# Tile-mode work of an attention + MoE kernel, regrouped: half of the next kv products ahead of the outputs, in one visit to the 64x64 tiles

## Chip, cores, metric

One core of one Trainium2 chip. The time is the device time of the slowest (here the only) core in microseconds, medians of several runs. "Slab" is one of nine blocks of 512 tokens; their lengths are read from traces. In the views PE is the tensor engine, PEld its weight loads, DVE the vector engine and ACT the scalar engine; PSUM, in banks 0 to 7, is where PE leaves its sums until another engine copies them out. "MoE products" are those of the reference's last two lines.

## The reference

```python
q_s = softmax(q, axis=-1); k_s = softmax(k, axis=2)          # per head, 8 x 8 heads, 576 x 64
kv  = einsum('bhsd,bhse->bhde', k_s, v)
x   = einsum('bhsd,bhde->bhse', q_s, kv)   -> [4608, 512]
h   = x @ w_in                                                # 512 -> 2048
out = (h * sigmoid(beta * h)) @ w_out                         # 2048 -> 512
```

## The kernel before

A list of operations is built in program order; each operation waits on semaphores for what it reads, writes and, by PSUM bank, touches. An operation signals if some later operation of another engine depends on it:

```python
for k in r:
    deps.extend(self.writer.get(k, ()))
    self.readers.setdefault(k, []).append(op)     # every reader is kept
for k in w:
    for d in self.readers.get(k, ()):             # so a later writer depends on every one
        if d is not op and not self._same(d, op):
            deps.append(d)
...
for op in self.ops:
    for d in op.deps:
        d.inc = True                              # and every one signals
```

Slab t is 64 MoE products x @ w_in, then 64 products with w_out (four groups u of 16), 128x512 each. Between them lie "visits" to the 64x64 tiles of the array, for attention: `kv_a` and `kv_b`, the two halves of kv of batch t+2 (36 products of 65 columns each, in PSUM banks 1 and 2), `out_quads`, the outputs of batch t+1 (8 products of 512 columns, banks 5, 6, 7, 0), and every second slab `outr_quads`, the remainders of two batches (16 products of 64 columns, again in banks 1 and 2).

```python
def block(b, kv):
    out_quads(b, (5, 6, 7, 0))
    if kv:
        kv_a(b + 1)
    else:
        outr_quads(b, (1, 2))
...                                  # (product of the slab after which it comes, what)
elif t == 1:
    todo = spread(outr_steps(1), 94, 95)
    todo += [(95, lambda: kv_a(2)), (103, lambda: kv_b(2)),
             (117, lambda: block(2, True)), (125, lambda: kv_b(3))]
elif t < 7 and t % 2 == 0:
    todo = [(80, lambda: block(t + 1, False))]
    if t + 2 < B:
        todo += [(93, lambda: kv_a(t + 2)), (101, lambda: kv_b(t + 2))]
elif t < 7:
    todo = [(93, lambda: block(t + 1, True)), (101, lambda: kv_b(t + 2))]
```

K and V are double buffered: exponentials of batch b+2 write the buffer that kv of batch b read. So all 72 kv products of batches up to 5 signal; batches 6 and 7 have no successor and signal only where a result is read. Outputs need QT, q after two transposing transfers.

The softmax here doesn't subtract the row's maximum and nothing guards it: scores larger than these inputs give would overflow.

## Time and profile before

| | before |
|---|---|
| time, median of 3 | 283.53 us (283.52 to 283.65) |
| span of the profiled run | 281.8 us |
| PE busy | 273.1 us, 97% |
| slabs 2, 3, 4, 5, 6, 7 | 29.60, 29.35, 29.45, 29.15, 28.41, 27.63 us |

A slab's length is the distance between the starts of two `XT,WIN` groups in the timeline of PE. How to read the rest stands in the prediction.

### The profile page before, as it was taken

How to read it: one execution, taken by the hardware profiler on the slowest of the kernel's cores; microseconds unless marked ns; L12 is line 12 of the kernel's file. 1: busy time of each engine (PE TensorE's matmuls, PEld its weight loads, DVE VectorE, ACT ScalarE, POOL GpSimd, SP SyncE). 2: the span in 40 equal slices, each digit the busy share in tenths (PEclk: the TensorE clock that was granted, in tenths of full speed). 3: DMA queues.
4: the chain of work that ended last, by engine and by line, in shares of the span. 5: the costliest groups of instructions: out<-in, count | busy, mean ns of one | idle time of the engine just before them, and what ended most of it. 6: DMA issues, size and time to landing. Idle time of an engine off the chain costs nothing.

```text
span 281.8 us, 4474 instructions
## 1 busy us (share of the span) xinstructions
PE 273.1 (97%) x1835; PEld 133.2 (47%) x1870; DVE 106.2 (38%) x211; ACT 168.6 (60%) x242; POOL 36.1 (13%) x56
## 2 busy tenths in 40 slices
PE   7899999999999999999999999999999999999995
PEld 3545454445445444544454444444444444444443
DVE  4764686308392337004651454043704100110012
ACT  5767788889467915794479527881761186017500
POOL 6630041116104030300040000000000000000000
PEclk9799999999999999999999999999999999999999
DMA  7999999999999999909970025000710020012022
GB/s 231 384 386 401 387 381 302 379 334 240 262 395 181 333 311 404 108 0 269 341 155 3 2 93 130 0 3 37 171 36 0 29 122 0 0 58 93 0 74 74
DMA packets 42044, 50.10 MB, mean 178 GB/s; under 512 B 20900, under 2 KB 29348, under 8 KB 40872
## 3 DMA queue, kind: packets, MB, share of 16 engines
q1 hardware_dynamic: 41072, 48.77, 57.6%
q10 hardware_dynamic: 952, 1.06, 1.1%
q8 instruction: 14, 0.23, 0.4%
q14 instruction: 6, 0.05, 0.0%
HBM read 36.71 MB, written 9.44 MB: 164 GB/s over the span
## 4 chain that ended last, share of the span: by engine, by line
PE 89%; ACT 4%; issue 2%; DVE 2%; DMA 1%; POOL 0%; ACTq 0%; POOLq 0%
PE PS L390 88%; ACT EQ L320 2%; DMA QF<-in_q_dram 1%; ACT L339 1%; PE PS L388 1%; ACT EK L339 1%; DVE QS L356 0%; POOL EQ L358 0%; ACT EQR L345 0%; ACT XT L540 0%; DVE KVD L428 0%; DVE EQ L358 0%; DVE KVC L527 0%; DVE RC L525 0%; DVE QI L357 0%
## 5 line engine op out<-in xcount | busy, mean ns | idle before, releaser
L723 ACT ACTIVATE GT<-PS,BETA 128x512 bf16<-128x512 f32 x144 | 96.8, 689 | 81.8 <-PE PS L390 81.8
L390 PE MATMUL PS<-WOUT,GT 128*128 128x512 bf16 (+2 forms) x569 | 126.8, 373 | 1.7 <-issue 0.5
L390 PE MATMUL PS<-XT,WIN 128*128 128x512 bf16 x565 | 125.8, 379 | 0.6
L390 PEld LDWEIGHTS PS<-XT,WIN 128*128 128x128 bf16 x576 | 60.6, 106 | 63.0 <-ACT GT L723 0.4
L390 PEld LDWEIGHTS PS<-WOUT,GT 128*128 128x128 bf16 x592 | 55.8, 98 | 63.0
L778 DVE COPY O2S<-PS 128x512 f32<-128x512 f32 x33 | 22.7, 688 | 97.0 <-PE PS L390 96.9
L375 POOL CAST VB<-VF 128x576 bf16<-128x576 f32 x29 | 20.8, 718 | 77.2 <-DMA VF<-in_v_dram 67.3
L356 DVE TENSOR_REDUCE QS<-EQ 128x8 f32<-128x512 bf16 (+1 forms) x22 | 20.0, 911 | 15.7 <-ACT EQ L320 15.7
L540 DVE CAST XT<-PS 128x512 bf16<-128x512 f32 x12 | 7.7, 686 | 33.8 <-PE PS L390 33.8
L320 ACT ACTIVATE EQ<-QF 128x512 bf16<-128x512 f32 x32 | 17.8, 616 | 1.7 <-DMA QF<-in_q_dram 1.5
L339 ACT ACTIVATE EK<-KF 128x1152 bf16<-128x1152 f32 (+1 forms) x16 | 15.9, 1035 | 1.7 <-DMA KF<-in_k_dram 1.5
L358 DVE TENSOR_TENSOR EQ<-EQ,QI 128x1024 bf16<-128x1024 bf16 (+1 forms) x14 | 16.0, 1146 | 0.5
L358 POOL TENSOR_TENSOR EQ<-EQ,QI 128x512 bf16<-128x512 bf16 x8 | 8.3, 1042 | 27.9 <-DVE QI L357 27.5
L390 PEld LDWEIGHTS PS<-VB,EK 64*64 64x64 bf16 x504 | 7.3, 109 | 5.2 <-issue 3.9
L540 ACT CAST XT<-PS 128x512 bf16<-128x512 f32 x12 | 6.3, 577 | 4.8 <-PE PS L390 4.8
L390 PE MATMUL PS<-VB,EK 64*64 64x65 bf16 x504 | 8.8, 195 | 0.0
L723 ACT ACT_TABLE_LOAD x5 | 6.4, 1283 | 0.1
L390 PE MATMUL PS<-XT 128*128 128x512 f32 x6 | 5.0, 1009 | 1.5 <-DVE XT L221 1.5
L332 ACT ACTIVATE EKD<-KF 64x576 bf16<-64x576 f32 (+1 forms) x6 | 5.0, 841 | 1.0 <-DMA KF<-in_k_dram 0.9
L525 DVE RECIPROCAL RC<-PS 128x2 f32<-128x2 f32 x12 | 2.0, 165 | 8.8 <-PE PS L390 8.8
L357 DVE RECIPROCAL QI<-QS 128x8 f32<-128x8 f32 (+1 forms) x22 | 5.0, 226 | 0.8
L339 ACT ACT_TABLE_LOAD x4 | 5.1, 1283 | 0.1
(62 smaller groups left out, 87.3 us busy)
## 6 DMA issues: line engine op xcount, KB each, us to landing
out_dram<-O2S SPq DMA_DIRECT2D x8, 1024.0 KB, 5.1
QF<-in_q_dram SPq DMA_DIRECT2D x30, 256.0 KB, 6.6
KF<-in_k_dram SPq DMA_DIRECT2D x6, 1152.0 KB, 8.5
VF<-in_v_dram SPq DMA_DIRECT2D x6, 1152.0 KB, 11.5
KF<-in_k_dram SPq DMA_DIRECT2D x8, 288.0 KB, 8.4
VF<-in_v_dram SPq DMA_DIRECT2D x8, 288.0 KB, 8.7
WST<-in_moe_w_in_dram SPq DMA_DIRECT2D x8, 256.0 KB, 8.3
O2S<-in_moe_w_in_dram SPq DMA_DIRECT2D x4, 512.0 KB, 11.9
```

The costliest lines, as they stand in the source:

```text
L320: add(ACTE, lambda e, o=o, a=a: e.activation(o, a, ACT.Exp), r=[("qf", i, hp)] if b < 2 else [("qf", i, hp, x) for x in ((2, 3) if hp % 2 ...
L332: add(ACTE, lambda e: e.activation(o, a, ACT.Exp), r=[("kf", i, h) for h in hps], w=[("ek", i, h, e_) for h in hps])
L339: add(ACTE, lambda e: e.activation(o, a, ACT.Exp), r=[("kf", i, h) for h in range(hp, hp + n)], w=[("ekc", i, h) for h in range(hp, hp + n)])
L356: add(DVE, lambda e: e.tensor_reduce(s_, a, AX.X, ALU.add), r=ks, w=[("qs", i, hp0)])
L357: add(DVE, lambda e: e.reciprocal(v_, s_), r=[("qs", i, hp0)], w=[("qi", i, hp0)])
L358: add(eng, lambda e: e.tensor_tensor(a, a, vb, ALU.mult), r=ks + [("qi", i, hp0)], w=ks)
L375: add(eng, lambda e: (e.copy if eng == ACTE else e.tensor_copy)(o, a), r=[("vf", i, hp), ("vone", i)], w=[("vb", i, hp, h) for h in ((0, 1 ...
L388: add(PE, lambda e: e.transpose(o, l, r_), r=r, w=w, bank=[bk])
L390: add(PE, lambda e: e.matmul(o, l, r_, start=start, stop=stop, tile_position=tp), r=r, w=w, bank=[bk])
L540: add(eng, lambda e, eng=eng, bk=bk, hp=hp: (e.copy if eng == ACTE else e.tensor_copy)(XT[i][:, hp, :], PS[bk][:, :]), r=[("ps", bk)], w=[ ...
L723: add(ACTE, lambda e: e.activation(GT[:, f, :], PS[bk][:, :], ACT.Silu, scale=BETA[:, f:f + 1]), r=[("ps", bk), "beta"], w=[("gt", f)], ba ...
L778: add(eng, lambda e: (e.copy if eng == ACTE else e.tensor_copy)(O2S[t % 2][:, u, :], PS[bk][:, :]), r=[("ps", bk)], w=[("o2", t % 2, u)], ...
```

## The change

The intent: fewer visits. In even slabs, outputs with remainders and each half of kv made three visits; now half of kv, outputs and remainders are one, and the other half follows 18 products on. In odd slabs and in slab 1 the number of visits stays and kv goes ahead of the outputs.

```diff
-        def block(b, kv):
+        def block(b):
+            if b + 1 < B:
+                kv_a(b + 1)
             out_quads(b, (5, 6, 7, 0))
-            if kv:
-                kv_a(b + 1)
-            else:
+            if b % 2 and b > 1:
                 outr_quads(b, (1, 2))
@@ t == 1
-                         (117, lambda: block(2, True)), (125, lambda: kv_b(3))]
+                         (116, lambda: block(2)), (124, lambda: kv_b(3))]
@@ t > 1
-            elif t < 7 and t % 2 == 0:
-                todo = [(80, lambda: block(t + 1, False))]
+            elif t < 7:
+                todo = [(94, lambda: block(t + 1))]
                 if t + 2 < B:
-                    todo += [(93, lambda: kv_a(t + 2)), (101, lambda: kv_b(t + 2))]
-            elif t < 7:
-                todo = [(93, lambda: block(t + 1, True)), (101, lambda: kv_b(t + 2))]
+                    todo += [(112, lambda: kv_b(t + 2))]
```

## The prediction

> **What bounds the kernel now**
>
> I read the page's busy shares first, then the chain that ended last, then the tensor engine's timeline from 45 us to the end, then narrow windows of its weight loads and of the vector engine.
>
> ```profile
> PE 273.1 (97%) x1835; PEld 133.2 (47%) x1870; DVE 106.2 (38%) x211; ACT 168.6 (60%) x242; POOL 36.1 (13%) x56
> ...
> PE 89%; ACT 4%; issue 2%; DVE 2%; DMA 1%; POOL 0%; ACTq 0%; POOLq 0%
> ```
>
> TensorE (PE) is busy for 97% of the span and is 89% of the chain; ACT, the next engine, is at 60%. A gain must come out of PE's own stream. The timeline of PE over slab 4, and the two ends of slab 7, which has no attention work in it:
>
> ```profile
> 136.31 13.98 PE L390 MATMUL PS<-XT,WIN 128*128 128x512 bf16 x63
> 150.13 3.40 PE L390 MATMUL PS<-WOUT,GT 128*128 128x512 bf16 x15
> 153.68 0.63 PE L390 MATMUL PS<-QT,KVC 64*64 64x512 bf16 x8
> 154.13 0.29 PE L390 MATMUL PS<-QTR,KVC 64*64 64x64 bf16 x16
> 154.36 2.98 PE L390 MATMUL PS<-WOUT,GT 128*128 128x512 bf16 x13
> 157.27 0.48 PE L390 MATMUL PS<-VB,EK 64*64 64x65 bf16 x36
> 157.91 1.67 PE L390 MATMUL PS<-WOUT,GT 128*128 128x512 bf16 x7 [0.16 <-issue]
> 159.51 0.48 PE L390 MATMUL PS<-VB,EK 64*64 64x65 bf16 x36
> 159.93 6.00 PE L390 MATMUL PS<-WOUT,GT 128*128 128x512 bf16 x26
> 165.76 13.98 PE L390 MATMUL PS<-XT,WIN 128*128 128x512 bf16 x63
> ...
> 223.32 13.98 PE L390 MATMUL PS<-XT,WIN 128*128 128x512 bf16 x63
> ...
> 250.95 13.98 PE L390 MATMUL PS<-XT,WIN 128*128 128x512 bf16 x63
> ```
>
> A line is a start, a length, a kind and a count. Slab 7 takes 250.95 - 223.32 = 27.63 us for 128 MoE products, so 0.2159 us each: no bubble. Slab 4 takes 165.76 - 136.31 = 29.45, so its three visits to the 64x64 tiles cost 1.82 us. Likewise from the slab starts in the same view (77.36, 106.96, 136.31, 165.76, 194.91, 223.32): slabs 2, 3, 5 and 6 pay 1.97, 1.72, 1.52 and 0.78. The "0.16 <-issue" is no wait: seven products are listed where eight weight loads stand, a record is missing.
>
> Per visit, with 0.2159 us per product: product 81 of slab 4 ought to start at 136.31 + 80 x 0.2159 = 153.58 and starts at 154.36, so outputs plus remainders cost 0.78. The two kv visits cost 0.52 and 0.51 (weight loads after them start at 157.68 and 159.92). In slab 5 outputs and half of kv share a visit: 0.99, then 0.52 for the other half.
>
> One real wait shows in slab 1, in the weight loads:
>
> ```profile
> 73.13 0.11 PEld L390 LDWEIGHTS PS<-QT,KVC 64*64 64x64 bf16 x4 [0.42 <-DMA QT<-EQ]
> 73.58 0.11 PEld L390 LDWEIGHTS PS<-QT,KVC 64*64 64x64 bf16 x4 [0.33 <-DMA QT<-EQ]
> ```
>
> All eight load within 0.14 us in slab 4. Here the second four stop until 73.58, for the second transposing transfer (issued 68.9, landing 4.6 us later). The 0.42 of the first four is the idle that stands before every visit, so no wait. And in the vector engine's timeline, the reader of the kv sums in slabs 2 and 4:
>
> ```profile
> 102.02 0.17 DVE L525 RECIPROCAL RC<-PS 128x2 f32<-128x2 f32 x1 [1.46 <-PE PS L390]
> ...
> 160.04 0.17 DVE L525 RECIPROCAL RC<-PS 128x2 f32<-128x2 f32 x1 [0.81 <-PE PS L390]
> ```
>
> Second halves start at 100.64 and 159.51, so the reader starts 1.38 and 0.53 us later: the same 36 products, signalled 0.85 us later in slab 2. In the code every product of kv up to batch 5 has a later writer of its K buffer in batch b+2, and so signals; batches 6 and 7 have none.
>
> **What the Trainium skill says**
>
> "TensorEngine Tiling (Array Packing)", Key Properties: changing the tiling mode, unlike the tile, drains TensorE. The trace agrees, with a small size. Going in: last wide product at 156.95 (157.167 - 0.216) to first kv product at 157.27 is 0.32, 0.10 over its stream. Going out: the group's 0.48 less one product's 0.19 puts the last kv start at 157.56, and the next wide weights load at 157.68: 0.12 for a product of 65 columns, that is some 0.10 over its stream (65/512 of 0.216 is 0.03). A visit's two switches cost about 0.20.
>
> "TensorE: Matmul & The Clock Gate", "The cost: per-tile semaphore tail": increments of tiled products serialize, 26.3 ns each. For 36 that estimates 0.95 us; the trace's 0.85 agrees.
>
> The same page, "Wait — 56ns, not 53.3ns?", has 215.7 ns between warm 512-column products; the trace's 215.9 agrees, so the MoE stream has nothing left to give.
>
> **The change part by part**
>
> No product, evacuation or transfer is added or removed; the instruction order shows only moves on PE, and one evacuation moved ahead on DVE in slabs 2, 4 and 6. In the steady slabs product 94 is followed by kv first half, outputs, and in even slabs remainders; product 112 by the other half of kv.
>
> Slabs 2 and 4: three visits become two. In slab 4 the joint visit is: entry 0.10, kv 0.32 (0.48 - 0.19 + one stream of 0.03), outputs 0.45 (153.68 to 154.13), remainders 0.10, exit 0.12: 1.09, against 0.78 + 0.52 = 1.30. Gain 0.21, which is one pair of switches. Slab 2: kv runs 0.08 slower (its group is 0.56 long), before as well as after: 0.20. There 60 signalling products now stand in one visit, and the tail might push back on PE; I take 0.18.
>
> Slabs 3 and 5: two visits before and after, only the order within turns. Slab 5 before: 0.99. After: 0.10 + 0.32 + outputs to exit (two streams of 0.216 plus 0.12) 0.55 = 0.97. Slab 3: 1.11 before (weight load after it at 128.15, due at 127.04), 0.10 + 0.40 + 0.55 = 1.05 after. Gains 0.02 and 0.06, inside what I can resolve: 0.05 together.
>
> Slab 6: one visit, moved from product 80 to 94: 0.
>
> Slab 1: its third visit costs 74.38 - 73.13 + 0.10 = 1.35, against 1.11 in slab 3, the difference being the wait for QT. After, the visit begins one product earlier (72.92) with kv: 0.40 of it, so outputs from 73.32 and their second four from 73.54, just about when the transfer lands. The wait of 0.23 goes, but for 0.04 or so, and the turned order gives 0.06: 0.25.
>
> Sum: 0.18 + 0.21 + 0.05 + 0.25 = 0.69 us. 283.53 - 0.69 = 282.84.
>
> **Do the operands come in time?** Visits now ask for kv operands first. Slab 1: VB of batch 3 is cast by 71.86 (four casts from 69.01), EK by 68.8, asked for at 72.9. Slab 2: EK of batch 4 ready at 95.6, asked for at 97.4. Slab 5: EK at 184.0, asked for at 186. Room of 1 to 2 us each. Other way round: kv's second half comes 11 products later, 16 before the slab's end. Its reader needs 1.38 + 0.9 us; the next slab reaches bank 1 after 16 + 4 products, 4.3 us. Outputs in even slabs come 14 products later, with 34 left (7.3 us) to evacuate. Evacuation of u = 1 queues behind those of outputs and remainders, some 4.3 us after the visit begins in slab 2 with the tail; its bank is wanted at 5.6.
>
> **The rivals**
>
> A. The switches are nearly free inside a burst, or the exit drain after 512-column outputs is dearer than after 65-column kv. For: I have entry and exit only to some 0.03 us, and tile products overlap. Against: three-visit slab 4 pays 0.30 more than slab 5, though it only has 16 tiny remainders more, whose stream is 0.10. Then only slab 1 gains: 283.2 to 283.4.
>
> B. The semaphore tail. 36 signalling kv products before the outputs delay the evacuations, by about 0.7 us, and might hold PE back or bring a bank late. For: the 0.85 in the trace. Against: the rooms above are over 1 us, and in slabs 4 and 5 kv signals little. It would give back 0.1 to 0.3 us: 282.9 to 283.2.
>
> C. A wait takes the place of the removed one: kv in front of outputs comes too early for K or V under a full DMA (9 tenths up to 134 us). Against: the rooms above. If it did, a wait of 1 us at one slab would give 283.8.
>
> D. A cascade from earlier output evacuations or transfers to something larger. Stores and loads are issued at the same places, PE's order sets their time, and PE moves by tenths: nothing to see.
>
> **Range and chances**
>
> The sum is 0.69; the doubtful terms are slab 1 (0.05 to 0.3, it hangs on a transfer's landing) and slab 2 with its tail (0 to 0.2), and 0.05 for slabs 3 and 5. That gives a gain of 0.25 to 1.0, so 282.5 to 283.3. The before runs spread over 0.13 us. Two per cent are 5.7 us, three quarters of all that the visits in slabs 2 to 6 cost together (7.81 us), so faster by 2% is out of reach; slower would need a stall of several us where I find room everywhere. Chances: 0.005 faster, 0.985 within, 0.01 slower.
>
> **What would show it**
>
> Slabs 2 and 4 shorter by 0.2 (29.4 and 29.25), 3 and 5 within 0.06, 6 and 7 unchanged; two visits with wide products around them in slabs 2 and 4. In slab 1 the eight output weights load together and no wait on QT remains. The XT evacuation starts later after its products in slabs 1 to 3 than in 4 and 5. I am wrong if wide products pause on VECTOR or ACT evacuations, if kv weight loads wait for VB or EK, or if slab 4 does not shorten though a switch pair is gone.

## More of the kernel before

One thing that I passed over then is in the page: the row of the granted clock has a 7 in its second slice.

```profile
PEclk9799999999999999999999999999999999999999
```

## The result

After: 282.90 us median of 4 (282.31 to 283.35), before 283.59 in the same rounds; ratio 0.9974, 95% interval 0.9952 to 0.9996. A ratio is the mean time of one kernel's fast runs over that of the other's in the same rounds, so not quite the ratio of the medians. By the bound of 2% the two are the same. The median moved by 0.69 us, the gain that was predicted. But two of the four runs had a granted clock of 1.00 (282.31 and 282.57) and two of 0.994 (283.35 and 283.23), so this median lies between two groups; the clocks of the four runs of before are not listed. And the traces do not divide the gain as the prediction did.

The page after, PE's timeline of slabs 2 and 4 after, and the remainders of slab 2 before:

```profile
PE 271.8 (97%) x1836; PEld 132.9 (47%) x1870; DVE 104.6 (37%) x211; ACT 169.0 (60%) x242; POOL 36.7 (13%) x56
...
PEclk9999999999999999999999999999999999999999
```

```profile
76.34 13.98 PE L390 MATMUL PS<-XT,WIN 128*128 128x512 bf16 x62
...
96.72 0.56 PE L390 MATMUL PS<-VB,EK 64*64 64x65 bf16 x36
97.12 0.69 PE L390 MATMUL PS<-QT,KVC 64*64 64x512 bf16 x8
97.55 0.54 PE L390 MATMUL PS<-QTR,KVC 64*64 64x64 bf16 x16
98.25 3.83 PE L390 MATMUL PS<-WOUT,GT 128*128 128x512 bf16 x17 [0.16 <-issue]
...
105.97 13.98 PE L390 MATMUL PS<-XT,WIN 128*128 128x512 bf16 x63
...
135.32 13.98 PE L390 MATMUL PS<-XT,WIN 128*128 128x512 bf16 x63
...
155.70 0.48 PE L390 MATMUL PS<-VB,EK 64*64 64x65 bf16 x36
156.01 0.60 PE L390 MATMUL PS<-QT,KVC 64*64 64x512 bf16 x8
156.45 0.29 PE L390 MATMUL PS<-QTR,KVC 64*64 64x64 bf16 x16
156.90 3.83 PE L390 MATMUL PS<-WOUT,GT 128*128 128x512 bf16 x17 [0.16 <-issue]
...
164.54 13.98 PE L390 MATMUL PS<-XT,WIN 128*128 128x512 bf16 x63
```

```profile
95.18 0.29 PE L390 MATMUL PS<-QTR,KVC 64*64 64x64 bf16 x16
```

Both slabs lost one visit. Slab 4 went from 29.45 to 29.22. Slab 2 took 105.97 - 76.34 = 29.63, where it had taken 29.60: it gained nothing. The place is to be seen: the same 16 remainder products last 0.54 us in slab 2 and 0.29 in slab 4 (and 0.29 in slab 2 before), and kv 0.56 and 0.48.

The two profiled spans differ by 1.3 us, which is more than the change can have made: 0.81 of it comes before any instruction that moved. The first slab begins its long run of MoE products at 16.60 before and at 15.79 after, with the same order of PE work up to there. The view of stretches, from before (columns: stretch, PE busy and its instructions, granted clock, transfers' share, GB/s) and the same stretch after:

```profile
10.00:11.00 1.00, 1.00 (x19) 0.50 1.03 406
```

```profile
10.00:11.00 1.00, 0.93 (x23) 1.00 1.03 403
```

In the profile of before the clock was at half speed from about 9.4 to 12.8 us (finer stretches of the same view; the expectation below says 9 to 12.4, which is misread); a second profile of the changed kernel had the same from about 10.7 to 14.1. So a pair of profiles has to be compared slab by slab, not by span.

The wait on QT in slab 1 was gone in this profile (all eight weights load in one go), but not in two later ones, as the experiments show:

```profile
72.49 0.34 PEld L390 LDWEIGHTS PS<-QT,KVC 64*64 64x64 bf16 x8
```

### The profile page after: what moved, and what is told of

Its sections match the earlier page's. It is cut to its first block, busy times and chain, and to the rows that moved or that the text cites. A ratio compares the mean times of both kernels' runs of the same rounds, so it can differ in the third digit from the quotient of the medians.

```text
span 280.5 us, 4478 instructions
## 1 busy us (share of the span) xinstructions
PE 271.8 (97%) x1836; PEld 132.9 (47%) x1870; DVE 104.6 (37%) x211; ACT 169.0 (60%) x242; POOL 36.7 (13%) x56
## 3 DMA queue, kind: packets, MB, share of 16 engines
q10 hardware_dynamic: 952, 1.06, 1.1%
## 4 chain that ended last, share of the span: by engine, by line
PE 84%; DMA 8%; SPq 3%; DVE 2%; issue 1%
PE PS L390 84%; DMA O2S<-in_moe_w_in_dram 4%; DMA O2S<-in_moe_w_out_dram 4%; SPq L645 1%; SPq L261 1%; DVE QS L356 1%; DVE WOUT L638 1%; SPq L251 0%; PE PS L388 0%; DVE WIN L649 0%; DVE KVC L527 0%; DVE RC L525 0%; DVE QI L357 0%; DVE O2S L799 0%
## 5 line engine op out<-in xcount | busy, mean ns | idle before, releaser
L375 POOL CAST VB<-VF 128x576 bf16<-128x576 f32 x29 | 21.5, 741 | 77.9 <-DMA VF<-in_v_dram 43.8
L390 PEld LDWEIGHTS PS<-VB,EK 64*64 64x64 bf16 x504 | 6.5, 107 | 5.9 <-issue 4.9
```

What stands on the lines that cost most here:

```text
L375: add(eng, lambda e: (e.copy if eng == ACTE else e.tensor_copy)(o, a), r=[("vf", i, hp), ("vone", i)], w=[("vb", i, hp, h) for h in ((0, 1 ...
L390: add(PE, lambda e: e.matmul(o, l, r_, start=start, stop=stop, tile_position=tp), r=r, w=w, bank=[bk])
```

## The experiments

Theory after the result: (1) a visit less is worth a pair of array switches; (2) in slab 2 the signals of 60 tiled products hold PE back and eat that; (3) slab 1's length hangs on when a transposing transfer lands; (4) the rest is the clock near the start. Rivals: the transfers, busy to nine tenths up to 134 us, slow slabs 2 and 3; the order inside a visit is what gains; the change itself keeps the clock up. Slab lengths from the traces, all in us; "slab 1, tail" runs from its first w_out product to slab 2:

| run | slab 1, tail | 2 | 3 | 4 | 5 | 6 |
|---|---|---|---|---|---|---|
| before | 17.18 | 29.60 | 29.35 | 29.45 | 29.15 | 28.41 |
| changed | 16.96 | 29.63 | 29.35 | 29.22 | 29.09 | 28.42 |
| changed, again | 17.09 | 29.63 | 29.36 | 29.21 | 29.10 | 28.41 |
| quiet changed | 18.01 | 29.22 | 29.09 | 29.22 | 29.10 | 28.41 |
| quiet before | 17.54 | 29.44 | 29.15 | 29.45 | 29.14 | 28.42 |
| loud changed | 17.90 | 29.63 | 29.36 | 29.63 | 29.35 | 28.41 |
| merged, old order | 17.57 | 31.30 | 29.35 | 31.22 | 29.14 | 28.42 |
| merged, kv in the middle | 17.40 | 29.89 | 29.35 | 29.33 | 29.15 | 28.41 |
| quiet, one visit more | 16.74 | 29.45 | 29.10 | 29.44 | 29.10 | 28.64 |
| slab 1 only | 16.97 | 29.60 | 29.35 | 29.45 | 29.14 | 28.41 |
| slab 1, outputs late | 16.95 | 29.60 | 29.35 | 29.45 | 29.14 | 28.42 |
| quiet, outputs late | 16.60 | 29.22 | 29.09 | 29.22 | 29.10 | 28.41 |
| the same, two more products | 16.60 | 29.22 | 29.09 | 29.22 | 29.09 | 28.42 |

In slabs 2 to 6 the same program repeats to 0.01 us, on different chips, so a difference of 0.03 there can be read. The tail of slab 1 cannot be read so. Several of these runs have the same program in slab 1 and differ only later: before and the two merged ones took 17.18, 17.57 and 17.40 there, the changed kernel, the same again and loud 16.96, 17.09 and 17.90, quiet changed and the one with a visit more 18.01 and 16.74. The three profiles of the changed kernel's slab 1 held PE's loads up for QT by nothing, 0.24 and 1.07 us in all.

### The changed kernel again

No edit.

> The changed kernel, unaltered, for more runs with their granted clocks. Slab theory (the change is worth what its slabs show, 0.47 us, and the rest of the 1.3 us between the two profiles is the clock that fell to 0.5 from about 9 to 12.4 us in the profile of before only, 0.81 us): its runs fall into two groups, near 282.4 with clock 1.00 and near 283.2 with clock 0.994, the kernel before has the same two groups about 0.5 higher (282.9 and 283.6), and like against like differs by 0.3 to 0.6. Rival (the change itself moves the kernel out of the slow group): before never shows clock 1.00, and this kernel does in half or more of its runs. Slabs in the profile: 2, 3, 4, 5 at 29.63, 29.35, 29.22, 29.09 us within 0.02.

Measured: 283.02 us median of 6, before 283.67 of 11, ratio 0.9979 (0.9963 to 0.9994). The slabs came out as expected. Over all fast runs of these two kernels whose clock is listed, mean clock 0.999 or more against 0.998 or less: before 283.31 (10 runs) and 283.83 (23 runs), changed 282.46 (4) and 283.17 (6). Like against like that is 0.85 and 0.66 (pooled over chips, so rough). Before, too, had runs at full clock: the rival that the change keeps the clock up is not supported, although 10 of 33 and 4 of 10 are too few to exclude a small effect. The expected 0.3 to 0.6 was too little, which pointed to slab 1.

### Quiet: only last readers signal

```diff
-            self.readers.setdefault(k, []).append(op)
+            rs = self.readers.setdefault(k, [])
+            if lean:                      # products on the 64x64 tiles
+                rs[:] = [d for d in rs if not d.lean]
+            rs.append(op)
```

The edit takes it that on PE the last reader, once done, speaks for those ahead of it; no trace here tests that by itself, but the results were correct. The kv visits now have 2 signals of 36, the joint ones 12 or 14 of 60.

> The changed kernel, in which of the products on the 64x64 tiles only the last reader of each operand signals (12 or 14 of the 60 of a joint visit where all 60 did, 2 of 36, 6 of 44)[...]. Tail theory (serialized signals hold PE back, and that ate the gain of slab 2): slabs 2 and 4 both take 29.2, slabs 3 and 5 both 29.1, slab 1 gets shorter by about 0.4, in all 1.0 to 1.1 us less than the changed kernel, and the reader of the kv sums starts 0.5 instead of 1.4 us after the first product. Rival (slabs 1 to 3 are slower because the transfers are busy then, 9 tenths up to 134 us): slabs 2 and 3 stay at 29.6 and 29.35, and the time stays within 0.1 us.

> The same made quiet in the kernel before. Tail theory: slab 2 from 29.60 to 29.45 (three visits as in slab 4), slab 3 from 29.35 to 29.15, slab 1 shorter by 0.3 to 0.4, in all about 0.7 us; and then the change, without signals, is worth 0.2 in each of slabs 2 and 4: quiet after beats quiet before by 0.7 to 0.85 us for like clock. Rival (transfers): nothing changes.

Measured: quiet changed 282.43 us (ratio to before 0.9964, 0.9949 to 0.9979), quiet before 283.01 (0.9981, 0.9966 to 0.9997). Slabs 2 and 4 now take the same 29.22, slabs 3 and 5 the same 29.1. The transfers were as busy as ever (a share of 0.94 from 90 to 100 us and 1.11 from 100 to 110, before 0.99 and 1.10), so they are not what slowed slabs 2 and 3. Of the times, quiet before met its expected 0.7 (0.66), though not as expected: its slabs 2 and 3 gave 0.16 and 0.20, and its slab 1, expected 0.3 to 0.4 shorter, had a tail 0.36 longer in the profile. Quiet changed was 0.58 below quiet before, not the expected 0.7 to 0.85. It gained 0.59 over the changed kernel that ran beside it in place of 1.0 to 1.1: the slabs 2 to 6 gave their 0.67, and slab 1, expected 0.4 shorter, had a tail 0.9 longer than in that run of the changed kernel. Its PE timeline shows why, and below it that the remainders of slab 2 are back at 0.29:

```profile
71.75 0.48 PE L394 MATMUL PS<-VB,EK 64*64 64x65 bf16 x36
73.23 0.89 PE L394 MATMUL PS<-QT,KVC 64*64 64x512 bf16 x8 [1.01 <-DMA QT<-EQ]
...
98.30 0.29 PE L394 MATMUL PS<-QTR,KVC 64*64 64x64 bf16 x16
```

PE came to the outputs earlier (full clock at the start, fewer signals), and stood 1.01 us until QT landed. The second load of weights then went at 73.71; it had gone at 73.58 before and at 73.50 in the changed kernel's second profile, but before 72.83 in its first. By issue and time to landing the second transposing transfer landed at 72.6 us in that first profile, at 73.6 in loud, with the same program and full clock up to there, and at 74.1 in quiet before, with the dip. So it is no fixed time, but differs by 1.0 us between like runs, and what PE gains ahead of this point it can lose here.

### Loud: signals added where there were none

```diff
+            op.inc = op.inc or op.loud          # loud: kv products of batches 6 and 7
```

> The changed kernel, in which all kv products of batches 6 and 7 signal as well (60, 36, 44 - 4, 36 signals in the visits of slabs 4 and 5, where 24, 2, 4, 2 were); nobody waits for the added ones. Tail theory: slab 4 rises from 29.22 to 29.6 and slab 5 from 29.09 to about 29.35, the values of slabs 2 and 3, so plus 0.6 to 0.7 us in the profile. Rival (transfers): both stay.

Measured: 283.81 us (single run), and slabs 4 and 5 at 29.63 and 29.35, within 0.01 of the lengths of slabs 2 and 3, though the transfers' share where these visits lie is 0.01 (155 to 165 and 185 to 195 us), against a full 1.06 from 90 to 100 us. PE's timeline of slab 4, loud:

```profile
156.55 0.56 PE L392 MATMUL PS<-VB,EK 64*64 64x65 bf16 x36
156.95 0.69 PE L392 MATMUL PS<-QT,KVC 64*64 64x512 bf16 x8
157.38 0.54 PE L392 MATMUL PS<-QTR,KVC 64*64 64x64 bf16 x16
```

Signals that nobody waits for cost 0.41 us in the joint visit of 60 with the visit of 36 behind it. Taking them away and putting them in agree: theory (2) is shown.

### Merged, but in the old order

Slabs 2, 4 and 6 of the kernel before in one visit: outputs, remainders, kv.

```diff
-            if kv:
-                kv_a(b + 1)
-            else:
+            if b % 2 and b > 1:
                 outr_quads(b, (1, 2))
+            if kv:
+                kv_a(b + 1)
...
-                todo = [(80, lambda: block(t + 1, False))]
+                todo = [(93, lambda: block(t + 1, t + 2 < B))]
```

> The kernel before, in which slabs 2, 4 and 6 make one visit of outputs, remainders and the first half of kv at product 93, in the order of before (kv last); slab 1 and the odd slabs as before. Theory (a visit less is the gain, the order within is worth little, and 60 signals in one visit eat it in slab 2): slab 4 at 29.2 to 29.25 as in the changed kernel, slab 2 within 0.05 of 29.6, slabs 3 and 5 at 29.35 and 29.15, slab 6 at 28.41. Rival (kv first is what gains): slab 4 stays near 29.45.

Measured: 287.27 us, 3.4 more than before, and I had not expected it. PE's timeline, and the vector engine's, in slab 2:

```profile
98.20 0.29 PE L390 MATMUL PS<-QTR,KVC 64*64 64x64 bf16 x16
99.98 0.81 PE L390 MATMUL PS<-VB,EK 64*64 64x65 bf16 x36 [1.49 <-DVE XT L556]
```

```profile
98.21 1.29 DVE L540 CAST XT<-PS 128x512 bf16<-128x512 f32 x2 [2.41 <-PE PS L390]
99.42 0.74 DVE L556 CAST XT<-PS 128x256 bf16<-128x256 f32 x2
```

kv and remainders share banks 1 and 2. With kv last it has to wait until the vector engine has copied the outputs and then the remainders: 1.49 us, twice. So the order is not free: in this kernel, a joint visit pays only if kv does not come behind the remainders. I had looked at these banks only for the second half of kv.

### Merged, kv in the middle

```diff
             if kv:
                 kv_a(b + 1)
-            else:
+            if b % 2 and b > 1:
                 outr_quads(b, (1, 2))
...
+                todo = [(93, lambda: block(t + 1, t + 2 < B))]       # kv_b at 112
```

> The kernel before, in which slabs 2, 4 and 6 make one visit in the order outputs, first half of kv, remainders, with the last half of kv at product 112; slab 1 and the odd slabs as before. Theory (the order matters only in that kv must not come after the remainders in banks 1 and 2, whose evacuation it would wait for): no pause inside the visit, slab 4 at 29.2 to 29.3, slab 2 at 29.6 to 29.7, slab 6 28.41. Rival (kv has to be first): a pause of some 0.5 us or more in slabs 2 and 4.

Measured: 283.03 us (single run), no pause. Slab 4 at 29.33, slab 2 at 29.89, a little over what was expected. Of the 0.23 that slab 4 gained in the changed kernel, 0.12 comes with this order too; kv first is worth the other 0.11. Slab 2, with its 60 signals, is worse than with three visits. Why kv first is 0.11 cheaper even with few signals I did not settle.

### One visit more

On the quiet changed kernel, remainders alone, nine products later.

```diff
-            if b % 2 and b > 1:
-                outr_quads(b, (1, 2))
...
+                if t % 2 == 0:
+                    todo += [(103, lambda: outr_quads(t + 1, (1, 2)))]
```

> The quiet version of the changed kernel, with the remainders moved out of the joint visit into one of their own nine products later, in slabs 2, 4 and 6: one visit more in each, the same work. Switch theory: each of the three slabs gets longer by 0.20 (29.42, 29.42, 28.61), slabs 3 and 5 stay at 29.09. Rival A of the prediction (switches inside bursts are nearly free, and something else made the gain of slab 4): under 0.05 each.

Measured: slabs 2, 4 and 6 are longer by 0.23, 0.22 and 0.23 us, with the same products; slabs 3 and 5 the same. Slab 6, whose visit is short, shows it bare:

```profile
214.33 0.63 PE L394 MATMUL PS<-QT,KVC 64*64 64x512 bf16 x8
214.89 2.12 PE L394 MATMUL PS<-WOUT,GT 128*128 128x512 bf16 x9
216.93 0.32 PE L394 MATMUL PS<-QTR,KVC 64*64 64x64 bf16 x16
217.18 5.57 PE L394 MATMUL PS<-WOUT,GT 128*128 128x512 bf16 x24
```

A visit more, with its pair of switches, costs 0.22 to 0.23 us in each of the three slabs, and quiet before against quiet changed (29.44 and 29.22, 29.45 and 29.22) says the same. Theory (1) is shown, rival A of the prediction is out.

### Slab 1 alone, and slab 1 with late outputs

Both on the kernel before, slabs 2 to 6 untouched; the first with the change's order in slab 1, the second:

```diff
-                         (117, lambda: block(2, True)), (125, lambda: kv_b(3))]
+                         (117, lambda: kv_a(3)),
+                         (123, lambda: (out_quads(2, (5, 6, 7, 0)), kv_b(3)))]
```

> The kernel before with the change in slab 1 alone (first half of kv of batch 3 ahead of the outputs of batch 2, one product earlier); slabs 2 to 6 as before. Theory (the change gains 0.25 from slabs 2 to 6 and the rest in slab 1, where kv fills part of the wait for the transposing transfer): slabs 2 to 6 at 29.60, 29.35, 29.45, 29.15, 28.41, and the median 0.2 to 0.5 below before. Rival (slab 1 is worth nothing, the wait is only moved): within 0.1 of before.

> The kernel before with slab 1's outputs of batch 2 six products later, beside the last half of kv, and nothing else (signals and slabs 2 to 6 as before). Theory: no weight load of the outputs waits on QT; the whole wait of slab 1 goes, 0.2 to 1.0 us by run, so the median is 0.6 to 1.0 below before, and the runs with clock 1.00 gain most. Rival (the wait is as small in all runs as the 0.23 in the one profile): 0.2 to 0.3.

Measured: slab 1 alone 283.34 us against 283.69 before (ratio 0.9984, 0.9965 to 1.0003), late outputs 283.20 (0.9983, 0.9960 to 1.0007). Both in the expected direction, the second short of the expected 0.6 to 1.0, and both intervals include no change. In the one profile of each no load is put down to QT: with slab 1 alone the eight weights go in one group from 73.06, with late outputs from 73.95. For slab 1 alone that can be a lucky landing, as in the changed kernel's first profile.

### Quiet, and the outputs of slab 1 late

The quiet changed kernel with `kv_a(3)` at 116 and outputs with `kv_b(3)` at 123.

> The quiet version of the changed kernel, with the outputs of batch 2 in slab 1 seven products later, into the visit of kv's last half (the number of visits is the same). Theory (the second transposing transfer lands at 73.2 to 73.7 us after the start whenever PE arrives, since the transfers are full then, so that wait takes back what PE gains earlier): no weight load of the outputs waits on QT by more than 0.15 us beyond the entry of a visit, slab 2 starts 0.5 to 1.0 earlier than with the wait (near 76.3 with a clock of 1.00 at the start, 77.0 with the dip), and the median is 0.3 to 0.8 us below the quiet changed kernel's 282.43. Rival (the transfers' landing follows PE, or the outputs are now late for slab 2): within 0.2 us of 282.43, or worse with waits on XT at the start of slab 2.

Measured: 281.33 us median of 6 (281.12 to 282.07), ratio to before 0.9919 (0.9902 to 0.9936), on another chip than the quiet changed kernel's 0.9964. It beats both kernels. The outputs' weights in slab 1, whose idle of 0.42 is the one before every visit:

```profile
74.77 0.14 PEld L394 LDWEIGHTS PS<-QT,KVC 64*64 64x64 bf16 x8 [0.42 <-issue]
```

The tail of slab 1 is 16.60 in this profile, which has the dip of the clock, and again 16.60 in the next experiment's, which has not; quiet changed had 18.01 and, in the run with a visit more, 16.74. With the outputs out of the way of the landing the tail is the same in both profiles: theory (3) is shown. More came of it than the 0.3 to 0.8 expected: 1.10 between the medians. With the wait away, what was saved earlier reaches the end: mean 281.24 at full clock (4 runs), 281.97 in the two others. In quiet changed the dip had cost nothing that shows: 282.56 at full clock (3 runs), 282.35 in the two others.

### The same with two more products near the start

```diff
         turn_beta()
+        warm(2, 0)                              # two 512-column products without use
```

> The same with two more 512-column products without use after the transposing of beta at some 8 us, where PE stood idle 0.5 us in the profile of before. Theory (the dip of the clock to 0.5 for 3.4 us around 9 to 14 us comes from a stretch with too little PE work, and where it falls is chance): no dip in the profile, all runs within 0.2 us of each other, median 0.2 to 0.6 below the late outputs alone. Rival (the dip does not hang on these gaps): as many slow runs as without, and up to 0.4 us lost.

Measured: 281.51 us median of 6 (281.12 to 282.34). The clock was 0.999 or 1.00 in all six runs, against four of six without; but the median is no better, and the mean of all six is 281.56 against 281.48. (One run, 282.34, lies 2.7 us above its span where most lie 1.8 above; by the spans the means are 279.57 and 279.68.) Perhaps filling the gap holds the clock (six runs are too few to say), but the gain, if any, is within the noise. Not worth keeping.

## Why the prediction was right, and where not

The time, 282.84 predicted and 282.90 measured, was right, and the main mechanism too; its division by slabs was partly wrong, and the sum agreed by some luck: slab 2 gave nothing, and the median made up for it by what came from slab 1 and by which clocks the few runs drew.

- **Slab 4, 0.21 for a pair of switches:** 0.23 measured, and 0.22 to 0.23 per pair when a visit was added. Right in size; of the 0.23, the run with kv in the middle puts 0.11 down to kv going first, which the prediction priced at 0.02 in slab 5 and not here.
- **Slab 2, 0.18:** this step failed. It allowed 0.02 for the tail of signals; the slab got 0.03 longer. The signals of its two visits, 60 and 36, cost 0.41 us against the quiet version (29.63 and 29.22), of which slab 2 had paid 0.16 already before (29.60 and 29.44). Rival B, put at 0.1 to 0.3 given back, is what happened, by way of PE itself and not of a late bank; I had read the late signals from the vector engine's reader, and not gone on to what a longer queue of them does to PE.
- **Slabs 3 and 5, 0.05 together:** 0.00 and 0.06. In slab 3 the tail took the 0.06.
- **Slab 6, 0:** 0.01 longer.
- **Slab 1, 0.25:** 0.22 between the first two profiles, 0.09 with the second profile of the changed kernel; over three profiles each, the same two programs took 17.18 to 17.57 and 16.96 to 17.90, so that 0.22 came so near to 0.25 is luck. That no wait on QT remains was wrong in two profiles of three. In the timed runs, slab 1 alone moved the median by 0.35, an interval that includes zero. The prediction named this term as the doubtful one, for the right reason.
- **The sum:** slabs 2 to 6 hold 145.96 - 145.71 = 0.25 us, not 0.44. With slab 1's 0.22 that is 0.47; the medians say 0.65 to 0.69. The rest is in slab 1, where the wait by run is larger than in the one profile that I sized it from, or it is noise: the runs do not settle which.
- **What I had not seen:** the dip of the clock near the start, 0.81 us between the two profiled runs and present in both kernels; and that it is partly hidden before (283.83 against 283.31 is 0.52). That a late PE waits less for QT in slab 1 explains this, and fits the 0.73 where that wait is gone (281.97 and 281.24), but it was not tested by itself. Rival C (kv in front comes too early for K or V) did not show: no load in the changed kernel waits for them.
- **The evacuations come later in slab 2, as forecast:** the copy of outputs starts 1.11 us after the first output product in slab 2 (98.23) and 0.46 in slab 4 (156.47), and no product of the MoE waits for it.

## What to carry to other kernels

Price a change of array tiling from a slab that has none, then count visits. But look at which bank the next group of products writes, since a group put behind another in the same bank can wait out that one's evacuation, which here was a pause of 1.49 us for a saving of 0.23. Let only the last product of a group signal: a signal on every small product delays its reader and, in a long burst, PE itself. And before you trust a difference between two profiles, see where it starts; a transfer that PE has to wait for further on can hide a gain as well as a loss, and where its landing differs by run, as here by 1.0 us, one profile does not size the wait.

## What the Trainium skill lacked or had wrong

- "TensorE: Matmul & The Clock Gate", "The cost: per-tile semaphore tail", gives the tail as a delay of the completion. It lacks that the backlog holds PE back: 36 signalling products of 65 columns made their visit 0.07 to 0.08 us longer (quiet before against before: 0.15 or 0.16 for the two in slab 2), and 60 with 36 behind them 0.41 us (loud against changed, slab 4: 29.63 and 29.22, with nobody waiting for the added signals). Its advice to signal on the last product alone, followed here for each operand's last reader, was worth 0.67 us in slabs 2 to 6 of the changed kernel.
- "TensorEngine Tiling (Array Packing)", "Key Properties", says that a change of mode drains the array and gives no size: here a visit's pair of switches cost 0.22 to 0.23 us in three slabs.
- "TensorE: Matmul & The Clock Gate", "Why this matters for your kernels", asks for no idle gaps above some 3 us between bursts. Here the clock fell to 0.50 for 3.4 us near the start of some runs, although the longest idle of PE between 6 and 12 us in that trace was 0.51 us (the page's "A second HAM failure mode: psum-queue depth-cycling" has small idles that do this, without a size). What set it off here is open: the stretch ahead of it also holds PE's transposes, and was not taken apart. The length agrees with the free-running window of 3.4 us in the same page's "What's actually happening", and so does it that the start differs by run (9.4 us and 10.7).
- No page says how long a transposing transfer takes when the other transfers fill the engines (rates are given, no such time): here 4.0 to 7.9 us from issue to landing in slab 1, with a landing that differs by 1.0 us between two runs with the same program up to there (72.6 and 73.6).
